# A rational activation spread over four engines: one product moved to GpSimd, two steps kept in PSUM

## The chip, the core and the metric

The kernel runs on one core of a Trainium2 chip. The metric is the device time of one execution in microseconds (us), lower is better. Matmuls run on TensorE (PE), elementwise work on VectorE (DVE), ScalarE (ACT) and GpSimd (POOL); transfers are issued from the queues of SyncE (SP) and GpSimd. Each engine works through its own instructions in the order in which they were issued, and waits on semaphores for the others.

## The reference

Three stages in a row, all in float32, for 8 batches of 3072 rows of 256 columns (24,576 rows):

```python
scores = (1.0 / S) * np.matmul(z, z.transpose(0, 2, 1))   # z: 8 x 3072 x 64
x = u * np.matmul(np.maximum(scores, 0.0) ** 2, v)        # attention, no softmax

# mixture of 8 experts, hidden width 1024: one expert per row, rows with x @ w_skip <= 0 pass through
h = np.maximum(xc[mask] @ w1[e], 0.0)
y[mask] = gate_w[mask, None] * (h @ w2[e])                # out = xc + y

# last stage, hidden width 2048: a rational activation
h = x @ w_in
P = a[0] + a[1] * h + a[2] * h**2 + a[3] * h**3
Q = 1.0 + np.abs(b[0]) * np.abs(h) + np.abs(b[1]) * h**2
out = (P / (Q + 1e-06)) @ w_out
```

## The kernel before

**Precision.** Matmuls take a rounded float32 form ("fp32r"). An operand is split into a high part (rounded) and a low part (the rest), and a product is the sum of three matmuls: high by high, high by low, low by high.

**Ticks and units.** Attention is cut into 8 x 12 x 12 = 1152 *ticks* (256 rows by 256 rows: scores, relu, square, split, product with V). Expert work and the last stage are cut into *units*: 256 hidden columns by 256 rows for an expert; 128 hidden columns by 512 rows for the last stage, which has 48 tiles of 16 units, 768 units in all. The batches are in five groups (1, 2, 2, 2, 1); when a group's attention is through, its expert units run, and its last-stage units are mixed with the ticks of the following groups. At the end there are no ticks left: 152 units of the last stage have the tag "y" (in `munits`, kind `kd`): 8 by themselves, 32 each beside one expert unit of the last group (tag "n"), 16 and then the 96 of the last group alone. Units mixed with ticks have the tag "x".

**One last-stage unit** (`plan_unit`), by the names of its steps. `h` is a PSUM bank of 128 x 512.

- l1a, l1b (TensorE): six matmuls into h (L1077).
- abs (ScalarE, L1257): u = |h|, in a buffer of the ring "mu". p1 (ScalarE, L1258): p = a3 h + a2, ring "mp".
- q0 (GpSimd L1264, or ScalarE L1262, or VectorE): q = b1 u + b0, ring "mq". q1 (VectorE or GpSimd, in the helper at L405): q = q u.
- p2 (VectorE, L1270): p = p h. p3 (VectorE, L1271): h = (p + a1) h, written back to PSUM.
- ln, ex (ScalarE, L1272, L1273): u = exp(-ln(q + CQ)), that is 1 / (q + CQ).
- gh (VectorE, L1274): the high part of the result, (h + a0) u, as fp32r, ring "mgh".
- v (VectorE, L1275): q = (q + CQ) gh. w (VectorE, L1277): q = (h + a0) - q, the rest of the numerator; after it the bank h is free.
- gl (GpSimd or VectorE, L405): the low part, q u, ring "mgl"; after it the buffers of mu and mq are free.
- l2h, l2l (TensorE): eight and four matmuls with gh and gl into the accumulator (L1095).

At the start of a tile its rows are transposed (L1130) and split (ScalarE L1136, VectorE L1139) into "mx"; at its end ScalarE copies the accumulators out (L1158). An expert unit (tag "n" beside a "y") has one pass on ScalarE (L1249) and one on VectorE (L1252).

**The order** is no hand-written list. `Flow.add` collects every step with a start position (the unit's position plus an offset from `LAG` plus a correction from `PAR`), the engines that may do it with a cost each ("D.602s|G1.245t": VectorE 0.602, else GpSimd 1.245), what it comes after, and which buffers of which ring it takes and frees. `Flow.run` plays this list forward at build time, always picks the engine that can begin earliest (within `SLIP` and `AHEAD`), and issues the instructions in that order. "s" and "t" behind a cost mark steps of VectorE and GpSimd which the planner doesn't let run at once.

**Rings that matter here** (`RINGS`): "b" has five PSUM banks (scores, h, transposes), "accA" one (the attention's accumulator; for the last group's experts theirs), "accM" two. "mu" has three buffers, "mp" two, "mq", "mgh" and "mgl" three. "T1" (six) holds attention's transposed z, "wr" (four) raw loads; both are of 128 x 512.

Of the kernel before, what the change touches and what calls it, by code (L numbers as in the profile page):

```python
# [25 lines left out]
    "T4tr.a": -3.5, "T4tr.s": -53.49, "T4tr.t": 16.24, "V.a": -66.78, "V.s": -77.95, "V.t": 93.99, "Vhi.a": -33.49,  # L26
    "Vhi.s": 12.36, "Vhi.t": -16.69, "Vld.a": -9.41, "Vld.s": 8.42, "Vld.t": 24.73, "W.2": 14.14, "W.f": -65.81,
    "W.n": -9.45, "W.v": -1.61, "Wh0.f": -3.7, "Wh1.f": -14.2, "Wl.f": -21.16, "Wo.f": 4.84, "abs.x": -57.27,
    "abs.y": -28.51, "avh.a": 10.74, "avh.t": 5.01, "avl.a": 3.11, "avl.t": -1.16, "ct.a": 71.47, "ct.t": -0.65,
    "ex.x": -7.74, "ex.y": -31.41, "gh.m": -0.03, "gh.n": -11.8, "gh.x": -11.19, "gh.y": -24.37, "gl.m": 122.35,  # L30
    "gl.n": -38.79, "gl.x": -6.33, "gl.y": 6.98, "hi.a": -61.05, "hi.t": -4.31, "l1a.m": 9.14, "l1a.n": 11.77,
    "l1a.x": 3.64, "l1a.y": 5.86, "l1b.m": 10.94, "l1b.n": 4.93, "l1b.x": 1.31, "l1b.y": 5.3, "l2h.m": 8.41,
    "l2h.n": 4.04, "l2h.x": 1.05, "l2h.y": 6.57, "l2l.m": 9.94, "l2l.n": -2.66, "l2l.x": -1.2, "l2l.y": 5.79,
    "ln.x": -3.21, "ln.y": 2.03, "lo.a": 3.28, "lo.t": -9.74, "mhi.1m": -50.66, "mhi.1n": -7.59, "mhi.2x": -7.05,
# [14 lines left out]
    "rt9.t": -93.95, "sq.a": -20.86, "sq.t": -0.93, "u.a": 20.74, "u.s": 47.17, "u.t": -38.96, "v.x": -14.79,  # L49
    "v.y": -38.17, "w.x": -101.31, "w.y": 1.28, "wsc.w": -7.4, "wsc1.f": -6.74, "wscc.w": -34.1, "wsch.w": -20.5,  # L50
    "wscl.w": 18.97,
# [3 lines left out]
SLIP = {"P": 8.95, "A": 0.25, "D": 24.11, "G": 5.02, "Q": 9.0}  # L55
LEAD, TAIL, POST, CARRY, MROW = 24, 8, 56, 1, 8
PE_TICK, PE_UNIT = 1.92, 2.87
# [13 lines left out]
class Flow:  # L71
# [7 lines left out]
    AHEAD = {"P": 10.76, "A": 4.45, "D": 125.36, "G": 8.71, "Q": 0.0}  # L79
# [138 lines left out]
def tile_attn_moe_moe2(  # L218
# [185 lines left out]
    def tt_on(e, *a, **k):  # L404
        (nc.vector if e == "D" else nc.gpsimd).tensor_tensor(*a, **k)  # L405
# [241 lines left out]
    def plan_tick(n):  # L647
# [47 lines left out]
        if ic == NIC - 1 and jp % 2 == 1:  # L695
            sf.append(("T1", ("T1", b, jp // 2)))
        add(at["S"], ("S", n), "P.476", scores, after=sd, takes=[("b", ("S", n))], frees=sf)
# [5 lines left out]
            at["avh"], ("avh", n), "P.952", lambda: av(st["hi"], (0, 1), True, False),  # L703
# [4 lines left out]
            at["avl"], ("avl", n), "P.476", lambda: av(st["lo"], (0,), False, True), after=[("lo", n), ("avh", n)],  # L708
# [499 lines left out]
    def plan_unit(t):  # L1208
        m, fp, xu, kd = munits[t]
        s = {}  # L1210
        ghb, glb = ("ah", "al") if kd == "n" else ("mgh", "mgl")
        flow.tag = kd
# [33 lines left out]
        add(at["l1a"], ("l1a", t), pl1, lambda: l1(0), after=prev + [("m", m.mi, h, "lo") for h in range(m.nh)] + [("W", wn)], takes=[hu])
        add(at["l1b"], ("l1b", t), pl1, lambda: l1(1), after=[("l1a", t)], frees=[("V" if kd == "n" else "mx", ("mx", m.mi))] if last else [])
        if m.kind == 1:
            add(at["gh"], ("gh", t), "A.478", lambda: act(buf("mgh", F32R), s["h"], AF.Relu), after=[("l1b", t)], takes=[(ghb, ("u", t))])  # L1249
            add(  # L1250
                at["gl"], ("gl", t), "D.602",
                lambda: stt(buf("mgl", F32R), s["h"], 0.0, s["gh"].bitcast(F32), op0=ALU.max, op1=ALU.subtract),  # L1252
                after=[("gh", t)], takes=[(glb, ("u", t))], frees=[hu],
            )
        else:

            pt("abs", "A.478", ["l1b"], lambda: act(buf("mu"), s["h"], AF.Abs), ["mu"])  # L1257
# [15 lines left out]
            pt("ex", "A.52", ["ln"], lambda: act(s["u"], s["u"], AF.Exp, scale=-1.0))  # L1273
            pt("gh", "D.663", ["ex", "p3"], lambda: stt(buf("mgh", F32R), s["h"], a0, s["u"], op0=ALU.add, op1=ALU.mult), ["mgh"])  # L1274
            pt("v", "D.602s", ["gh"], lambda: stt(s["q"], s["q"], CQ, s["gh"].bitcast(F32), op0=ALU.add, op1=ALU.mult))  # L1275
            add(
                at["w"], ("w", t), "D.663", lambda: stt(s["q"], s["h"], a0, s["q"], op0=ALU.add, op1=ALU.subtract),  # L1277
                after=[("v", t)], frees=[hu],
            )
# [6 lines left out]
            at["l2l"], ("l2l", t), "P.476", lambda: l2(1),  # L1286
# [191 lines left out]
```

## Time and profile before

| what | value |
|---|---|
| median of 3 runs | 5582.74 us (5581.83 to 5587.68) |
| profiled execution | 5577.05 us, of which the span of instructions 5575.3 |
| busy share of the span: PE, DVE, ACT, POOL | 96%, 81%, 75%, 55% |
| mean granted TensorE clock | 0.994 |
| instructions | 107,018 |

The page's busy shares are means over a span with stages that are limited by different engines; the views below cut it by time. The profiled execution is one run, somewhat faster than the median of the three.

### The profile page before, as it was taken

The numbers are of one execution on the slowest core, as the hardware profiler recorded it, in microseconds if no ns is written. First come the engines' busy times: TensorE is split into PE (matmuls) and PEld (weight loads), VectorE is DVE, ScalarE is ACT, GpSimd is POOL, SyncE is SP. The second block draws the span as 40 slices with busy tenths as digits, with TensorE's granted clock in tenths as the row PEclk, the third lists the DMA queues.
The fourth block names the chain that finished last, engine by engine and source line by source line (L and its number), as shares of the span: only waits on it lengthen the run. The fifth ranks groups of instructions, "written<-read, shape, count | busy, mean of one in ns | idle before, by whom it ended". The sixth has DMA issues, their size and how long they took to land.

```text
span 5575.3 us, 107018 instructions
## 1 busy us (share of the span) xinstructions
PE 5362.4 (96%) x39525; PEld 5027.9 (90%) x39525; DVE 4533.8 (81%) x7470; ACT 4202.2 (75%) x7663; POOL 3090.5 (55%) x4422
## 2 busy tenths in 40 slices
PE   9989999999999999999999999999999999999887
PEld 8989999999899999999899989999988888888666
DVE  6765777774498999899459999999638999998998
ACT  8866888885388888888448888888627888855776
POOL 3433445443256655665235566556526667765887
PEclk9999999999999999999999999999999999999999
DMA  4375111114510110112541010011351000044000
GB/s 136 115 273 218 64 51 42 34 53 176 176 60 32 45 40 31 31 41 76 178 154 36 32 50 27 29 32 48 132 207 63 24 25 20 25 157 140 16 16 17
DMA packets 205545, 435.31 MB, mean 78 GB/s; under 512 B 30094, under 2 KB 129017, under 8 KB 181458
## 3 DMA queue, kind: packets, MB, share of 16 engines
q1 hardware_dynamic: 177746, 360.66, 19.1%
q0 software_dynamic: 27264, 67.71, 3.5%
q8 instruction: 313, 5.13, 0.4%
q14 instruction: 222, 1.82, 0.1%
HBM read 308.56 MB, written 153.22 MB: 83 GB/s over the span
## 4 chain that ended last, share of the span: by engine, by line
PE 70%; DVE 13%; ACT 6%; DMA 4%; issue 4%; POOL 3%; SPq 0%; DVEq 0%; ACTq 0%; POOLq 0%
PE accA L684 24%; PE h L1077 17%; PE accM L1095 16%; PE S L661 4%; PE S L662 4%; DVE mq L1275 3%; DVE mgh L1274 3%; DMA mr<-xs 2%; DVE h L1271 2%; DVE mq L1277 2%; DVE mp L1270 1%; PE lp L773 1%; PE mt L1130 1%; ACT mp L1258 1%; ACT mu L1272 1%
## 5 line engine op out<-in xcount | busy, mean ns | idle before, releaser
L1077 PE MATMUL h<-mx,W 128*128 128x512 f32 x5760 | 1540.7, 400 | 64.1 <-DVE mq L1277 58.9
L684 PE MATMUL accA<-V,ah 128*128 128x256 f32 x9216 | 1270.0, 280 | 13.1 <-ACT ah L409 8.3
L405 POOL TENSOR_TENSOR mgl<-mq,mu 128x512 fp32r<-128x512 f32 x655 | 892.1, 1363 | 692.9 <-DVE mq L1277 395.8
L1077 PEld LDWEIGHTS h<-mx,W 128*128 128x128 f32 x5760 | 1013.5, 190 | 250.6 <-DVE mq L1277 75.3
L684 PEld LDWEIGHTS accA<-V,ah 128*128 128x128 f32 x9216 | 1164.4, 189 | 31.5 <-ACT ah L409 14.5
L1095 PE MATMUL accM<-W,mgh 128*128 128x256 f32 x7680 | 1054.5, 280 | 10.6 <-DVE mgh L1274 6.6
L1095 PEld LDWEIGHTS accM<-W,mgh 128*128 128x128 f32 x7680 | 979.6, 189 | 32.3 <-DVE mgh L1274 8.9
L676 DVE TENSOR_TENSOR al<-S,ah 128x512 fp32r<-128x512 f32 x1152 | 786.3, 683 | 168.4 <-ACT ah L409 143.9
L665 ACT ACTIVATE S<-S 128x512 f32<-128x512 f32 x1152 | 677.9, 588 | 119.2 <-PE S L662 109.5
L684 PE MATMUL accA<-V,al 128*128 128x256 f32 x4608 | 729.7, 281 | 5.9 <-DVE al L676 5.7
L1264 POOL TENSOR_SCALAR mq<-mu,coef 128x512 f32<-128x512 f32 x554 | 458.0, 827 | 473.1 <-ACT mu L1257 467.6
L668 ACT ACTIVATE S<-S 128x512 f32<-128x512 f32 x1152 | 676.0, 587 | 21.8
L1270 DVE TENSOR_TENSOR mp<-mp,h 128x512 f32<-128x512 f32 x768 | 522.3, 680 | 187.0 <-ACT mp L1258 178.1
L1257 ACT ACTIVATE mu<-h 128x512 f32<-128x512 f32 x768 | 458.0, 596 | 271.0 <-PE h L1077 212.2
L409 ACT ACTIVATE ah<-S 128x512 fp32r<-128x512 f32 x996 | 594.9, 598 | 63.3 <-PE accA L684 41.7
L1095 PE MATMUL accM<-W,mgl 128*128 128x256 f32 x3840 | 615.1, 282 | 27.9 <-POOL mgl L405 27.3
L1274 DVE SCALAR_TENSOR_TENSOR mgh<-h,coef,mu 128x512 fp32r<-128x512 f32 x768 | 571.3, 744 | 80.2 <-ACT mu L1273 64.9
L684 PEld LDWEIGHTS accA<-V,al 128*128 128x128 f32 x4608 | 621.4, 189 | 13.5 <-DVE al L676 8.2
L1275 DVE SCALAR_TENSOR_TENSOR mq<-mq,mgh 128x512 f32<-128x512 f32 x768 | 617.4, 805 | 15.7 <-DVE mgh L1274 0.5
L1272 ACT ACTIVATE mu<-mq 128x512 f32<-128x512 f32 x768 | 483.3, 629 | 179.1 <-POOL mq L405 138.6
L1258 ACT ACTIVATE mp<-h,coef 128x512 f32<-128x512 f32 x768 | 595.5, 775 | 23.3 <-DVE h L1271 18.8
L1095 PEld LDWEIGHTS accM<-W,mgl 128*128 128x128 f32 x3840 | 537.3, 189 | 63.4 <-POOL mgl L405 39.7
(157 smaller groups left out, 8466.9 us busy)
## 6 DMA issues: line engine op xcount, KB each, us to landing
W<-wsc SPq DMA_DIRECT2D x96, 1024.0 KB
wsc<-W SPq DMA_DIRECT2D x32, 1024.0 KB
W<-wsc POOLq DMA_DIRECT2D x32, 1024.0 KB
Wv<-wsc SPq DMA_DIRECT2D x64, 512.0 KB
vr<-in_v_dram SPq DMA_DIRECT2D x96, 256.0 KB
xs<-in_u_dram SPq DMA_DIRECT2D x96, 256.0 KB
x<-xs SPq DMA_DIRECT2D x96, 256.0 KB
mr<-x SPq DMA_DIRECT2D x96, 256.0 KB
```

Source lines behind the costliest of these rows:

```text
L405: (nc.vector if e == "D" else nc.gpsimd).tensor_tensor(*a, **k)
L409: act(out, in_, AF.Copy)
L665: act(st["s"], st["s"], AF.Relu, scale=1.0 / S)
L668: act(st["s"], st["s"], AF.Square)
L676: ttt(st["lo"], st["s"], st["hi"].bitcast(F32), op=ALU.subtract)
L684: mm(accs[b, ic][:, it * TT : (it + 1) * TT], lhsT=a[:, jj * TT + it * P : jj * TT + (it + 1) * P], rhs=VV[b, jp][:, vi, jj * D : (jj + 1) ...
L1077: mm(h, lhsT=lw, rhs=rw, start=(k == 0 and i == 0), stop=(k == NK - 1 and i == 2), skip_group_check=True)
L1095: mm(accs_[it // 2][:, it % 2 * TT : (it % 2 + 1) * TT], lhsT=(gh, gl)[part][:, it * P : (it + 1) * P], rhs=w[i][:, 512 + ff * D : 512 + ( ...
L1258: pt("p1", "A.664", ["l1b"], lambda: act(buf("mp"), s["h"], AF.Identity, scale=a3, bias=a2), ["mp"])
L1270: pt("p2", "D.602", ["p1", "abs"], lambda: ttt(s["p"], s["p"], s["h"], op=ALU.mult))
L1274: pt("gh", "D.663", ["ex", "p3"], lambda: stt(buf("mgh", F32R), s["h"], a0, s["u"], op0=ALU.add, op1=ALU.mult), ["mgh"])
L1275: pt("v", "D.602s", ["gh"], lambda: stt(s["q"], s["q"], CQ, s["gh"].bitcast(F32), op0=ALU.add, op1=ALU.mult))
```

## The change

For units of tag "y" alone:

- v goes from VectorE to GpSimd. GpSimd's instruction only multiplies, so the addition of CQ gets a pass of its own, qc, on ScalarE, ahead of ln.
- q1 may only be done by GpSimd.
- w writes its result to h in PSUM, no longer to q; so q is free after w.
- gl is done by VectorE, from h (PSUM) and u; after it h and u are free.
- u takes its buffer from the ring "T1" and q from the ring "wr".
- in the last group, every sixth unit takes its bank h from "accA".

Further, every cost that the planner uses for TensorE's steps, the offsets for "y", its limits `SLIP` and `AHEAD`, and all values of `PAR` are new, so the order of all work may differ.

```diff
-SLIP = {"P": 8.95, "A": 0.25, "D": 24.11, "G": 5.02, "Q": 9.0}
+SLIP = {"P": 11.41, "A": 0.25, "D": 8.5, "G": 24.05, "Q": 9.0}
-PE_TICK, PE_UNIT = 1.92, 2.87
+PE_TICK, PE_UNIT = 1.87, 2.8
-    "y": {"hc": 2.2, "l1a": 0.0, "l1b": 1.46, "abs": 3.3, "p1": 2.17, "q0": 3.9, "q1": 5.31, "p2": 3.21, "p3": 5.4, "ln": 8.99, "ex": 11.23, "gh": 11.96, "v": 13.69, "w": 14.84, "gl": 15.6, "l2h": 20.23, "l2l": 23.37},
+    "y": {"hc": 2.2, "l1a": 0.0, "l1b": 1.4, "abs": 2.9, "p1": 3.5, "q0": 3.6, "q1": 4.6, "p2": 4.4, "p3": 5.2, "qc": 6.1, "ln": 6.8, "ex": 7.5, "gh": 8.2, "v": 9.1, "w": 10.6, "gl": 11.4, "l2h": 12.5, "l2l": 14.5},
-    AHEAD = {"P": 10.76, "A": 4.45, "D": 125.36, "G": 8.71, "Q": 0.0}
+    AHEAD = {"P": 11.11, "A": 4.42, "D": 137.59, "G": 8.94, "Q": 0.0}
...
+        home = {"mgh": ghb, "mgl": glb}
+        if kd == "y":
+            home.update(mu="T1", mq="wr")
...
-        hu = ("b", ("u", t))
+        hb = "accA" if kd == "y" and m.g == NG - 1 and (t - len(munits)) % 6 == 0 else "b"
+        hu = (hb, ("u", t))
...
-            pt("q1", "D.602s|G1.245t", ["q0"], lambda e: tt_on(e, s["q"], s["q"], s["u"], op=ALU.mult))
+            pt("q1", "G1.245t" if kd == "y" else "D.602s|G1.245t", ["q0"], lambda e="G": tt_on(e, s["q"], s["q"], s["u"], op=ALU.mult))
...
+            if kd == "y":
+                pt("qc", "A.52", ["q1"], lambda: act(s["q"], s["q"], AF.Identity, bias=CQ))
+                pt("ln", "A.52", ["qc"], lambda: act(s["u"], s["q"], AF.Ln))
+                pt("ex", "A.52", ["ln"], lambda: act(s["u"], s["u"], AF.Exp, scale=-1.0))
+                pt("gh", "D.663", ["ex", "p3"], lambda: stt(buf("mgh", F32R), s["h"], a0, s["u"], op0=ALU.add, op1=ALU.mult), ["mgh"])
+                pt("v", "G1.245t", ["gh"], lambda: pool_tt(s["q"], s["q"], s["gh"].bitcast(F32), op=ALU.mult))
+                pt("w", "D.663", ["v"], lambda: stt(s["h"], s["h"], a0, s["q"], op0=ALU.add, op1=ALU.subtract), (), ["mq"])
+                pt("gl", "D.602", ["w"], lambda: ttt(buf("mgl", F32R), s["h"], s["u"], op=ALU.mult), ["mgl"], ["mu"], [hu])
+            else:
...

```

## Rows read from the trace of the kernel before

**Rows 1.** The page: busy time of TensorE, share of the span, instructions.
```profile
PE 5362.4 (96%) x39525; PEld 5027.9 (90%) x39525; DVE 4533.8 (81%) x7470; ACT 4202.2 (75%) x7663; POOL 3090.5 (55%) x4422
```

**Rows 2.** Windows: stretch, its length, busy us of each engine, clock, DMA.
```profile
0.00:4905.00 4905.00, 4795.72 (x35930) 4535.97 (x35930) 3918.05 (x6602) 3763.41 (x6953) 2586.78 (x3975) 1.00 0.24 79
1600.00:2600.00 1000.00, 992.45 (x7472) 938.46 (x7471) 912.50 (x1517) 850.87 (x1565) 607.93 (x896) 1.00 0.12 38
3000.00:4000.00 1000.00, 988.99 (x7414) 937.83 (x7413) 919.57 (x1525) 855.25 (x1562) 605.07 (x861) 1.00 0.14 44
4905.00:4940.00 35.00, 29.04 (x162) 24.59 (x162) 32.73 (x54) 19.97 (x35) 26.55 (x40) 0.90 0.42 144
4940.00:5127.00 187.00, 179.59 (x1315) 168.73 (x1316) 160.46 (x231) 101.55 (x169) 97.63 (x99) 0.99 0.52 173
5127.00:5565.00 438.00, 357.78 (x2120) 298.54 (x2119) 422.54 (x586) 316.19 (x505) 379.50 (x310) 0.98 0.05 17
5200.00:5550.00 350.00, 286.51 (x1686) 237.66 (x1686) 338.09 (x469) 257.52 (x412) 308.78 (x252) 0.98 0.05 17
```

**Rows 3.** The chain that ended last, 5200 to 5550 us: shares by line.
```profile
by line: DVE mq L1275 19.4%; DVE mgh L1274 17.3%; issue 15.3%; DVE h L1271 8.8%; DVE mp L1270 6.3%; DVE mq L1277 6.3%; ACT mp L1258 5.1%; ACT mu L1273 5.0%; ACT mu L1272 4.4%; PE h L1077 3.4%; PE accM L1095 3.3%; POOL mq L405 2.0%; PE mt L1
```

**Rows 4.** Groups of VectorE, 5200 to 5550 us: busy us, mean ns, idle before.
```profile
L1275 DVE SCALAR_TENSOR_TENSOR mq<-mq,mgh 128x512 f32<-128x512 f32 x91 | 93.1, 1023 | 3.7
L1274 DVE SCALAR_TENSOR_TENSOR mgh<-h,coef,mu 128x512 fp32r<-128x512 f32 x92 | 68.8, 748 | 6.1 <-ACT mu L1273 1.0
L1271 DVE SCALAR_TENSOR_TENSOR h<-mp,coef,h 128x512 f32<-128x512 f32 x92 | 68.6, 745 | 0.8
L1277 DVE SCALAR_TENSOR_TENSOR mq<-h,coef,mq 128x512 f32<-128x512 f32 x92 | 68.1, 740 | 0.0
L1270 DVE TENSOR_TENSOR mp<-mp,h 128x512 f32<-128x512 f32 x92 | 62.1, 675 | 1.3 <-ACT mp L1258 1.3
L1139 DVE TENSOR_TENSOR mx<-mt,mx 128x512 fp32r<-128x512 f32 x10 | 6.8, 682 | 0.0
```

**Rows 5.** Groups of ScalarE, 5200 to 5550 us.
```profile
L1273 ACT ACTIVATE mu<-mu 128x512 f32<-128x512 f32 x91 | 57.5, 632 | 2.9
L1272 ACT ACTIVATE mu<-mq 128x512 f32<-128x512 f32 x92 | 57.5, 625 | 48.7 <-POOL mq L405 48.7
L1257 ACT ACTIVATE mu<-h 128x512 f32<-128x512 f32 x91 | 54.0, 594 | 21.4 <-POOL mgl L405 12.3 <-PE h L1077 9.0
L1262 ACT ACTIVATE mq<-mu,coef 128x512 f32<-128x512 f32 x24 | 19.6, 817 | 0.8
```

**Rows 6.** Groups of GpSimd, 5200 to 5550 us.
```profile
L405 POOL TENSOR_TENSOR mgl<-mq,mu 128x512 fp32r<-128x512 f32 x92 | 133.5, 1451 | 7.2 <-DVE mq L1277 7.2
L405 POOL TENSOR_TENSOR mq<-mq,mu 128x512 f32<-128x512 f32 x92 | 125.6, 1376 | 4.8
L1264 POOL TENSOR_SCALAR mq<-mu,coef 128x512 f32<-128x512 f32 x68 | 54.3, 799 | 30.0 <-ACT mu L1257 30.0
```

**Rows 7.** Waits, 5200 to 5550 us: us in total, times, longest.
```profile
PE h L1077 <- DVE mq L1277: 40.5, 52, 2.1
...
ACT mu L1257 <- POOL mgl L405: 12.3, 30, 0.4
```

**Rows 8.** Timeline of one round, 5483 to 5497 us: start, duration, instruction.
```profile
5485.40 1.27 POOL L405 TENSOR_TENSOR mq<-mq,mu 128x512 f32<-128x512 f32 x1
5485.60 1.62 DVE L1275 SCALAR_TENSOR_TENSOR mq<-mq,mgh 128x512 f32<-128x512 f32 x1
...
5485.73 1.66 PE L1077 MATMUL h<-mx,W 128*128 128x512 f32 x6 [0.68 <-DVE mq L1277]
5486.63 1.77 POOL L405 TENSOR_TENSOR mgl<-mq,mu 128x512 fp32r<-128x512 f32 x1
...
5488.62 1.31 POOL L405 TENSOR_TENSOR mgl<-mq,mu 128x512 fp32r<-128x512 f32 x1 [0.22 <-DVE mq L1277]
...
5490.54 0.69 DVE L1275 SCALAR_TENSOR_TENSOR mq<-mq,mgh 128x512 f32<-128x512 f32 x1
```

More of the change, by code (lines that the diff above doesn't have):

```diff
@@ L22 @@
 PAR = {
[3 rows of a table removed]
[L26 to L34, printed above, removed]
[14 rows of a table removed]
-    "rt9.t": -93.95, "sq.a": -20.86, "sq.t": -0.93, "u.a": 20.74, "u.s": 47.17, "u.t": -38.96, "v.x": -14.79,
@@ L50 @@
-    "v.y": -38.17, "w.x": -101.31, "w.y": 1.28, "wsc.w": -7.4, "wsc1.f": -6.74, "wscc.w": -34.1, "wsch.w": -20.5,
-    "wscl.w": 18.97,
[3 rows of a table added]
+    "T4tr.a": -1.8, "T4tr.s": -47.01, "T4tr.t": 16.76, "V.a": -69.94, "V.s": -64.87, "V.t": 123.29, "Vhi.a": -23.69,
+    "Vhi.s": -5.03, "Vhi.t": -10.78, "Vld.a": -11.47, "Vld.s": 9.8, "Vld.t": 24.79, "W.2": 15.33, "W.f": -68.79,
+    "W.n": 16.29, "W.v": 1.9, "Wh0.f": -4.83, "Wh1.f": -0.1, "Wl.f": -36.74, "Wo.f": -23.32, "abs.x": -71.17,
+    "abs.y": 0.38, "avh.a": 5.32, "avh.t": 4.27, "avl.a": 1.39, "avl.t": -1.13, "ct.a": 80.47, "ct.t": 17.69,
@@ new lines @@
+    "ex.x": -9.49, "ex.y": -10.28, "gh.m": 2.4, "gh.n": -19.15, "gh.x": -12.57, "gh.y": 8.16, "gl.m": 137.7,
+    "gl.n": -50.97, "gl.x": -3.03, "gl.y": 0.79, "hi.a": -76.03, "hi.t": -4.81, "l1a.m": 8.89, "l1a.n": 9.5,
+    "l1a.x": 3.31, "l1a.y": 6.16, "l1b.m": 10.9, "l1b.n": -2.11, "l1b.x": 0.96, "l1b.y": 3.26, "l2h.m": 6.58,
+    "l2h.n": 4.9, "l2h.x": 0.84, "l2h.y": 11.51, "l2l.m": 8.95, "l2l.n": 0.11, "l2l.x": -1.98, "l2l.y": 5.31,
+    "ln.x": -3.09, "ln.y": 2.23, "lo.a": -20.21, "lo.t": -10.69, "mhi.1m": -13.94, "mhi.1n": -22.71, "mhi.2x": -7.11,
[14 rows of a table added]
@@ L52 @@
+    "rt9.t": -90.19, "sq.a": -29.62, "sq.t": -0.7, "u.a": 8.1, "u.s": 45.54, "u.t": -41.33, "v.x": -14.39, "v.y": -3.41,
+    "w.x": -117.81, "w.y": 2.62, "wsc.w": -5.9, "wsc1.f": -10.91, "wscc.w": -45.45, "wsch.w": -59.53, "wscl.w": 14.6,
 }
@@ L696, in plan_tick @@
             sf.append(("T1", ("T1", b, jp // 2)))
-        add(at["S"], ("S", n), "P.476", scores, after=sd, takes=[("b", ("S", n))], frees=sf)
+        add(at["S"], ("S", n), "P.467", scores, after=sd, takes=[("b", ("S", n))], frees=sf)
         add(at["relu"], ("relu", n), "A.478", relu, after=[("S", n)])
@@ L702, in plan_tick @@
         add(
-            at["avh"], ("avh", n), "P.952", lambda: av(st["hi"], (0, 1), True, False),
+            at["avh"], ("avh", n), "P.932", lambda: av(st["hi"], (0, 1), True, False),
             after=[("hi", n), ("V", b, jp)] + ([("avl", n - 1)] if n else []),
@@ L707, in plan_tick @@
         add(
-            at["avl"], ("avl", n), "P.476", lambda: av(st["lo"], (0,), False, True), after=[("lo", n), ("avh", n)],
+            at["avl"], ("avl", n), "P.466", lambda: av(st["lo"], (0,), False, True), after=[("lo", n), ("avh", n)],
             frees=[("ah", n), ("al", n)] + ([("V", ("V", b, jp))] if ic == NIC - 1 else []),
@@ L1215, in plan_unit @@
         first, last, ff = fp == 0, fp == m.nfp - 1, fp % 2
-        hu = ("b", ("u", t))
+        hb = "accA" if kd == "y" and m.g == NG - 1 and (t - len(munits)) % 6 == 0 else "b"
+        hu = (hb, ("u", t))
         def l1(half):
             if half == 0:
-                s["h"] = bank("b", f"h{t}")
+                s["h"] = bank(hb, f"h{t}")
             if m.nh == 1:
@@ L1234, in buf, with pt @@
         def buf(tag, dt=F32):
-            o = s[tag[1:]] = tl({"mgh": ghb, "mgl": glb}.get(tag, tag), f"{tag}{t}", dt)
+            o = s[tag[1:]] = tl(home.get(tag, tag), f"{tag}{t}", dt)
             return o
-        def pt(n, ops, after, fn, takes=(), frees=()):
+        def pt(n, ops, after, fn, takes=(), frees=(), more=()):
             add(
                 at[n], (n, t), ops, fn, after=[(a, t) for a in after],
-                takes=[(r, ("u", t)) for r in takes], frees=[(r, ("u", t)) for r in frees],
+                takes=[(home.get(r, r), ("u", t)) for r in takes],
+                frees=[(home.get(r, r), ("u", t)) for r in frees] + list(more),
             )
         prev = [("l1a", t - 1)] if t else []
-        pl1 = "P.714" if m.nh == 1 else "P.69"
+        pl1 = "P.7" if m.nh == 1 else "P.696"
         add(at["l1a"], ("l1a", t), pl1, lambda: l1(0), after=prev + [("m", m.mi, h, "lo") for h in range(m.nh)] + [("W", wn)], takes=[hu])
@@ L1268, in plan_unit @@
             pt("q0", "G.78|A.707|D.46s", ["abs"], q0, ["mq"])
-            pt("q1", "D.602s|G1.245t", ["q0"], lambda e: tt_on(e, s["q"], s["q"], s["u"], op=ALU.mult))
+            pt("q1", "G1.245t" if kd == "y" else "D.602s|G1.245t", ["q0"], lambda e="G": tt_on(e, s["q"], s["q"], s["u"], op=ALU.mult))
             pt("p2", "D.602", ["p1", "abs"], lambda: ttt(s["p"], s["p"], s["h"], op=ALU.mult))
             pt("p3", "D.663", ["p2", "abs"], lambda: stt(s["h"], s["p"], a1, s["h"], op0=ALU.add, op1=ALU.mult), (), ["mp"])
-            pt("ln", "A.52", ["q1"], lambda: act(s["u"], s["q"], AF.Ln, bias=CQ))
@@ L1273, in plan_unit @@
[L1273 to L1279, printed above, removed]
@@ L1280, in plan_unit @@
-            pt("gl", "G1.245t|D.602s", ["w"], lambda e: tt_on(e, buf("mgl", F32R), s["q"], s["u"], op=ALU.mult), ["mgl"], ["mu", "mq"])
+            if kd == "y":
[7 more added lines that the diff above has]
+            else:
+                pt("ln", "A.52", ["q1"], lambda: act(s["u"], s["q"], AF.Ln, bias=CQ))
+                pt("ex", "A.52", ["ln"], lambda: act(s["u"], s["u"], AF.Exp, scale=-1.0))
+                pt("gh", "D.663", ["ex", "p3"], lambda: stt(buf("mgh", F32R), s["h"], a0, s["u"], op0=ALU.add, op1=ALU.mult), ["mgh"])
+                pt("v", "D.602s", ["gh"], lambda: stt(s["q"], s["q"], CQ, s["gh"].bitcast(F32), op0=ALU.add, op1=ALU.mult))
+                add(
+                    at["w"], ("w", t), "D.663", lambda: stt(s["q"], s["h"], a0, s["q"], op0=ALU.add, op1=ALU.subtract),
+                    after=[("v", t)], frees=[hu],
+                )
+                pt("gl", "G1.245t|D.602s", ["w"], lambda e: tt_on(e, buf("mgl", F32R), s["q"], s["u"], op=ALU.mult), ["mgl"], ["mu", "mq"])
@@ L1281, in plan_unit @@
         add(
-            at["l2h"], ("l2h", t), "P.952", lambda: l2(0), after=[("gh", t)] + ([("l2l", m.ts[fp - 1])] if fp else []),
+            at["l2h"], ("l2h", t), "P.932", lambda: l2(0), after=[("gh", t)] + ([("l2l", m.ts[fp - 1])] if fp else []),
             takes=[(acc_tag(m), ("m", m.mi, h)) for h in range(m.nh)] if first else [],
@@ L1285, in plan_unit @@
         add(
-            at["l2l"], ("l2l", t), "P.476", lambda: l2(1),
+            at["l2l"], ("l2l", t), "P.466", lambda: l2(1),
             after=[("gl", t), ("l2h", t)] + ([("wsc1", wn)] if wn in range(E * FP1) and w_last[wn] == t else []),
```

34 rows, old and new, of the table PAR are left out of this document.

## The prediction, made before the changed kernel ran

> **What bounds the kernel now.** I read the page first: TensorE is busy in 96% of the span [rows 1]. That is an average over stages, so I cut the span where the work changes [rows 2]. Up to 4905 us attention and expert work run together, and TensorE idles for 109 us of 4905 (4905 - 4795.7). The units that the diff touches, those of tag "y", are the last 152 of 768 rational units: 8 alone (about 4905 to 4940), 32 each beside one unit of the last expert group (to about 5127), and 112 alone up to the end. In the middle piece TensorE is busy for 179.6 of 187 us, so there it is the bound. In the last piece it is busy for 357.8 of 438 us, and VectorE for 422.5.
>
> I take 5200 to 5550 us as the steady part of it: VectorE 338.1 of 350 us, GpSimd 308.8, TensorE 286.5, ScalarE 257.5 [rows 2]; 92 units pass in it (the counts of four of VectorE's five groups, [rows 4]). So a unit takes 350 / 92 = 3.80 us, of which VectorE works 3.675. The chain of waits agrees: its largest shares there are VectorE's, L1275 (v) first with 19.4% [rows 3]. TensorE does wait, 40.5 us at the first matmul of a unit, for L1277, the instruction that gives back a PSUM bank [rows 7]; but that instruction is late because VectorE is full.
>
> Why VectorE is full stands in its groups [rows 4]: p2 0.675, p3 0.745, gh 0.748, w 0.740 and v 1.023 us. v is as wide as the others. The timeline shows what it costs apart from its own work [rows 8]: one v that begins 0.20 us behind a GpSimd product takes 1.62 us, and the next GpSimd product takes 1.77; another v, that waits for nothing, takes 0.69. Products of GpSimd that met no v took 1.27 and 1.31. p2, which reads PSUM and SBUF, averages 0.675 with the same GpSimd work running, so it isn't held.
>
> **The change, step by step** (for a unit alone).
>
> *VectorE.* v leaves: -1.023. gl comes to VectorE. It isn't there in these units now; its nearest rows are p2, the same operation with one operand in PSUM and one in SBUF, 0.675, and the split at L1139 with an fp32r output, 0.682 [rows 4]. I take 0.68. w writes PSUM instead of SBUF: L1271 does that at 0.745, against L1277's 0.740, so nothing. The sum of means is now 0.675 + 0.745 + 0.748 + 0.740 + 1.023 + 0.074 (L1139, 6.8 us over 92 units) = 4.005, and the engine is busy for 3.675, so neighbours overlap by 0.33 a unit. Afterwards it is 4.005 - 1.023 + 0.68 = 3.66, less 0.33 = 3.33 us. Bounds: with no v that waits, all five may overlap by about 0.08 (3.26); if p2-p3 and w-gl stand back to back, where the second needs the first's result, those two overlap nothing (3.41).
>
> *GpSimd.* gl leaves, v comes: the same kind of product, both operands in SBUF. q1 was on GpSimd for 92 of 92 units already. No VectorE instruction with two tensors in SBUF is left in a unit, so the products should fall from 1.451 and 1.376 [rows 6] to about 1.29: busy time 308.8 / 92 = 3.36 becomes 3.36 - 0.16 - 0.09 = 3.11 us. If the lengthening stays, 3.36.
>
> *ScalarE.* One pass more, qc. The Ln with a constant added takes 0.625, q0 on ScalarE with its two columns of coefficients 0.817 [rows 5]; qc has one constant, so 0.625. Busy time 257.5 / 92 = 2.80 becomes 3.34 (0.08 overlaps), or 3.54 at the other price. ScalarE now does q0 in 24 of 92 units; each that goes back to GpSimd moves 0.82 there. Evened out, both stand at some 3.22.
>
> *What hides what.* So VectorE goes from 3.675 to 3.33 and stays the bound, but with two engines close below it, where now they have 0.3 and 0.9 us of slack. Now VectorE idles 0.13 us a unit. I take 0.17 afterwards, since ScalarE (five to six instructions in order) no longer has room to catch up: 3.50 us a unit. With 0.06 and 3.26 it is 3.32; with 0.25 and 3.41 it is 3.66.
>
> *Buffers.* A bank of the unit is given back after gl instead of after w, and the path to there gets qc. What a unit does while it holds the bank is now 1.66 (its matmuls, [rows 8]) + 0.594 + 0.799 + 1.376 + 0.625 + 0.632 + 0.748 + 1.023 + 0.740 = 8.2 us; five banks at 3.80 us a unit allow 19. Afterwards: with products at 1.29, 1.66 + 0.594 + 0.799 + 1.29 + 0.625 + 0.625 + 0.632 + 0.748 + 1.29 + 0.745 + 0.68 = 9.7 us, and five banks at 3.50 allow 17.5. In the last 96 units every sixth takes the attention's bank, which is worth six banks: 21. mu moves from three buffers to six ("T1"), mq from three to four ("wr"); both rings are the attention's, which by then issues no ticks, so I cost the move at nothing. No DMA is added or moved. v now stands in GpSimd's queue; behind it are q0 and q1 of later units and, in the middle piece, the scatters of the expert tiles, for which ScalarE's qc and the output tiles wait; there GpSimd is busy for only 97.6 of 187 us.
>
> *The sum.* The 438 us hold 113 units, counted as above. 113 x (3.80 - 3.50) = -34 us. In the two pieces ahead, TensorE idles 6.0 and 7.4 us, which bounds the gain at 13; I take -4, since in the 187 us VectorE isn't the bound. The last unit's chain gets qc (+0.6), and v and gl change engines at no net cost: +1. The two lists of start positions are also new for all other work. How much the order alone can do I bound by two stretches of the same mixture: 1600 to 2600 leaves TensorE idle for 7.6 us, 3000 to 4000 for 11.0 [rows 2], that is 3.4 us in 1000, or +-17 over 4905; no reason for a sign, so 0. Sum: -37 us. The profiled execution took 5577.05 us around a span of 5575.3, the median of the runs is 5582.74; the sum is a difference, so it goes to the median: **5546 us**. Alone the likeliest case ranges from 113 x 0.48 + 4 = -58 to 113 x 0.14 = -16, narrowed to 5530 to 5566 because both ends need all terms at once.
>
> **Rivals.**
>
> *Full packing.* VectorE's queue is filled without gaps at 3.30 us a unit, and the pieces ahead give 8: -64, 5519. For it: no instruction of VectorE waits for a GpSimd one to end. Against it: three engines above 3.2.
>
> *GpSimd becomes the bound.* If ScalarE can't take any q0, GpSimd has 2 x 1.29 + 0.80 = 3.38 clean, or 2 x 1.376 + 0.80 = 3.55 at today's lengthened product; with 0.13 idle 3.68, so 113 x 0.12 = -14: 5569. For it: v takes twice what it takes on VectorE when nothing is beside it (1.29 against 0.69, [rows 8]). The Trainium skill's GPSIMD Engine Reference, section 4.1, says the same as a rule: a two-input elementwise operation belongs on VectorE, GpSimd being about twice as slow. By that rule alone moving v loses 0.6 us a unit; the trace agrees with the ratio. Against it as a loss: the rows price v on VectorE at 1.023, not 0.69, and gl comes back from GpSimd in exchange.
>
> *The order elsewhere, or the gaps, take it back.* At 3.75 us a unit with a new order worth nothing, or at 3.60 with +17: about 5580, no change to be measured.
>
> *Slower: the bank.* Today a unit spends 19 - 8.2 = 10.8 us of its hold on waits in queues. If these grow with the number of hand-overs (GpSimd's v between two VectorE instructions, qc between GpSimd and ScalarE: nine steps become eleven), the hold is 9.7 + 13.2 = 22.9 us. On six banks that is 3.82 a unit, on five 4.58: over 96 and 17 units, 2 + 13 = +15 us: 5598. It decides from a hold of 6 x 3.80 = 22.8 us on. Against it: queues are long now because VectorE is full, and mu's three buffers, for which ScalarE's first pass waits [rows 7], become six.
>
> **How the numbers follow.** Likeliest case 0.52, full packing 0.17, GpSimd the bound 0.13, no change 0.09, slower 0.09. The first three are faster by more than 0.2% (11 us, about what a measurement here can tell from no change): 0.82, less 0.01 for their slow ends: 0.81 faster, 0.10 same, 0.09 slower. The range of 5520 to 5578 us reaches from full packing to the edge of no change; outside are half of full packing, the slower case and part of the unchanged one.
>
> **What would show it.** Right: in the steady part VectorE still has the highest busy share, some 95%, at about 3.5 us a unit; gl on VectorE near 0.68 and w near 0.745; GpSimd's two products near 1.29, none near 1.7; ScalarE above 90%; TensorE's wait for a bank now ends on gl. Wrong: products still at 1.4 (something else of VectorE holds GpSimd), gl or w well above 0.75, VectorE below 90% while TensorE waits for gl longer than 40 us (the bank), or a gain or loss that lies ahead of 4905 us (the order).

## The result, and the profile after

The changed kernel takes 5535.45 us (median of 4 runs); the kernel before, run again beside it, has a median of 5583.42. One of the four runs took 6764.53 us at a mean granted TensorE clock of 0.719; it is in that median but not in the ratio, and the other three took 5530.0 to 5538.0. The ratio is 0.991 with a 95% interval of 0.989 to 0.9929: 0.9% faster, 48 us, where 37 were forecast. A second series gave 5530.63 against 5586.91, ratio 0.990 (0.9884 to 0.9917).

The profiled execution took 5530.01 us with a span of 5528.3, that is 47.0 less than the span before. Four instants in TensorE's timeline split the difference: the last matmul of a tick, the first and the last of the last group's expert units, and the last of all.

| stretch | before, us | after, us | difference |
|---|---|---|---|
| start to the last tick's matmul | 4896.3 | 4911.2 | +14.9 |
| to the first expert unit of the last group | 35.6 | 38.9 | +3.3 |
| beside those expert units | 199.6 | 190.0 | -9.6 |
| lone units, to the last matmul | 433.9 | 377.8 | -56.1 |

So the lone units gave more than the whole gain, and some of it was lost ahead of them. The first instant in both profiles, the kernel before first (start, duration):

```profile
4895.63 0.62 PE L684 MATMUL accA<-V,al 128*128 128x256 f32 x4
```

```profile
4910.55 0.62 PE L683 MATMUL accA<-V,al 128*128 128x256 f32 x4
```

The windows after (columns as in [rows 2]; the third and fourth lines are the two lower stretches of the table, the last a steady part of the lone units):

```profile
0.00:4905.00 4905.00, 4787.04 (x35825) 4532.41 (x35826) 3933.89 (x6588) 3743.91 (x6897) 2608.91 (x3994) 1.00 0.23 79
4911.20:4950.00 38.80, 30.35 (x174) 26.54 (x173) 33.06 (x56) 26.59 (x48) 31.45 (x45) 0.87 0.27 84
4950.00:5140.00 190.00, 187.44 (x1404) 177.96 (x1403) 148.13 (x229) 126.99 (x216) 120.18 (x116) 1.00 0.56 187
5140.00:5518.00 378.00, 333.40 (x2083) 292.13 (x2081) 369.80 (x581) 351.03 (x607) 353.08 (x315) 1.00 0.06 20
5175.00:5500.00 325.00, 289.94 (x1800) 254.00 (x1799) 319.33 (x499) 308.62 (x535) 308.50 (x275) 1.00 0.06 19
```

In the steady part 98 units pass in 325 us (the count of gh below): 3.32 us a unit, against 3.80. VectorE is busy for 319.3 of 325 us (98%), ScalarE and GpSimd for 95% each; before, these three were at 97%, 74% and 88% [rows 2]. Beside the expert units TensorE is busy for 187.4 of 190 us; before, for 179.6 of 187.

The groups of 5175 to 5500 us (line, engine, operation, count, busy us, mean ns, idle before), first VectorE with gh, p3, w, p2 and gl, then ScalarE's qc, then GpSimd's q1, v and q0:

```profile
L1283 DVE SCALAR_TENSOR_TENSOR mgh<-h,coef,mu 128x512 fp32r<-128x512 f32 x98 | 72.9, 743 | 2.1 <-ACT mu L1282 1.8
L1277 DVE SCALAR_TENSOR_TENSOR h<-mp,coef,h 128x512 f32<-128x512 f32 x98 | 73.3, 748 | 0.8
L1285 DVE SCALAR_TENSOR_TENSOR h<-h,coef,mq 128x512 f32<-128x512 f32 x97 | 72.8, 751 | 0.0
L1276 DVE TENSOR_TENSOR mp<-mp,h 128x512 f32<-128x512 f32 x98 | 66.3, 677 | 2.7 <-ACT mp L1264 2.7
L1286 DVE TENSOR_TENSOR mgl<-h,mu 128x512 fp32r<-128x512 f32 x97 | 66.0, 681 | 0.1
...
L1280 ACT ACTIVATE mq<-mq 128x512 f32<-128x512 f32 x98 | 60.9, 621 | 2.9 <-POOL mq L404 2.5
L1268 ACT ACTIVATE mq<-mu,coef 128x512 f32<-128x512 f32 x20 | 16.1, 806 | 0.0
...
L404 POOL TENSOR_TENSOR mq<-mq,mu 128x512 f32<-128x512 f32 x99 | 128.0, 1298 | 5.8 <-ACT mq L1268 2.0
L1284 POOL TENSOR_TENSOR mq<-mq,mgh 128x512 f32<-128x512 f32 x97 | 126.2, 1302 | 8.1 <-DVE mgh L1283 8.1
L1270 POOL TENSOR_SCALAR mq<-mu,coef 128x512 f32<-128x512 f32 x79 | 61.7, 781 | 4.8 <-ACT mu L1263 4.8
```

Compare with [rows 4, 6]: no row of VectorE is above 0.76 us any more, and GpSimd's products are at 1.30 instead of 1.38 and 1.45. The waits of the same stretch show that TensorE hardly waits for a bank any more, 5.7 us instead of 40.5 [rows 7], and waits longer for gl as an operand, 28.2 us instead of 11.8:

```profile
PE accM L1094 <- DVE mgl L1286: 28.2, 30, 2.1
...
PE h L1076 <- DVE mgl L1286: 5.7, 5, 1.5
```

The timeline (start, duration) shows GpSimd's q1 and v back to back, with VectorE's gl and p2 beside them, neither side lengthened:

```profile
5486.55 1.30 POOL L404 TENSOR_TENSOR mq<-mq,mu 128x512 f32<-128x512 f32 x1
5486.55 0.74 DVE L1283 SCALAR_TENSOR_TENSOR mgh<-h,coef,mu 128x512 fp32r<-128x512 f32 x1
...
5487.21 0.68 DVE L1286 TENSOR_TENSOR mgl<-h,mu 128x512 fp32r<-128x512 f32 x1
...
5487.81 0.68 DVE L1276 TENSOR_TENSOR mp<-mp,h 128x512 f32<-128x512 f32 x1
5487.81 1.30 POOL L1284 TENSOR_TENSOR mq<-mq,mgh 128x512 f32<-128x512 f32 x1
```

### The profile page after: what moved, and what is told of

The parts are those of the page before. It is cut to its first block, busy times and chain, and to the rows that moved or that the text cites. A ratio compares the mean times of both kernels' runs of the same rounds, so it can differ in the third digit from the quotient of the medians.

```text
span 5528.3 us, 106807 instructions
## 1 busy us (share of the span) xinstructions
PE 5344.4 (97%) x39525; PEld 5034.9 (91%) x39525; DVE 4491.1 (81%) x7460; ACT 4254.6 (77%) x7776; POOL 3119.6 (56%) x4471
## 4 chain that ended last, share of the span: by engine, by line
PE 73%; DVE 14%; ACT 5%; issue 3%; POOL 3%; DMA 2%; SPq 0%; DVEq 0%; POOLq 0%; ACTq 0%
PE accA L683 24%; PE h L1076 18%; PE accM L1094 17%; PE S L660 4%; PE S L661 4%; DVE mp L1276 2%; DVE h L1277 2%; DVE mq L1291 2%; DVE mgh L1290 1%; DVE h L1285 1%; PE accM L1084 1%; PE h L1065 1%; PE lp L772 1%; DMA wr<-in_moe_w_dram 1%; PE mt L1129 1%
## 5 line engine op out<-in xcount | busy, mean ns | idle before, releaser
L1076 PE MATMUL h<-mx,W 128*128 128x512 f32 x5760 | 1522.5, 398 | 21.6 <-DVE mq L1293 11.8
L683 PEld LDWEIGHTS accA<-V,ah 128*128 128x128 f32 x9216 | 1168.4, 189 | 24.4 <-ACT ah L408 11.8
L404 POOL TENSOR_TENSOR mgl<-mq,mu 128x512 fp32r<-128x512 f32 x484 | 655.5, 1356 | 627.2 <-DVE mq L1293 380.7
L408 ACT ACTIVATE ah<-S 128x512 fp32r<-128x512 f32 x971 | 579.9, 597 | 47.2 <-PE accA L683 22.2
L661 PE MATMUL S<-T,T 128*128 128x256 f32 x2304 | 590.3, 281 | 0.0
L1277 DVE SCALAR_TENSOR_TENSOR h<-mp,coef,h 128x512 f32<-128x512 f32 x768 | 572.8, 747 | 3.8
L404 POOL TENSOR_TENSOR mq<-mq,mu 128x512 f32<-128x512 f32 x405 | 541.2, 1338 | 40.4 <-ACT mq L1268 15.4
```

Of the source, the lines that this page charges most:

```text
L408: act(out, in_, AF.Copy)
L661: mm(o, lhsT=lw, rhs=T4[b, ic], start=False, stop=(jj == 1), skip_group_check=True)
L683: mm(accs[b, ic][:, it * TT : (it + 1) * TT], lhsT=a[:, jj * TT + it * P : jj * TT + (it + 1) * P], rhs=VV[b, jp][:, vi, jj * D : (jj + 1) ...
L1076: mm(h, lhsT=lw, rhs=rw, start=(k == 0 and i == 0), stop=(k == NK - 1 and i == 2), skip_group_check=True)
```

## The experiments

In each, the planner lays out the order anew, so the edit is followed by a slightly or strongly different order. The planner's numbers stay those of the changed kernel, or of the kernel before, and aren't made anew for the edit; part of a loss can therefore be the order's, as the runs under "Steps or numbers?" show. Times a unit are counted by gh between 5200 and 5500 us unless another stretch is named. The five runs with a time but no ratio are single executions.

**Is it the PSUM operand?** gl from two SBUF tensors, everything else as changed:

```diff
-pt("w", "D.663", ["v"], lambda: stt(s["h"], s["h"], a0, s["q"], op0=ALU.add, op1=ALU.subtract), (), ["mq"])
-pt("gl", "D.602", ["w"], lambda: ttt(buf("mgl", F32R), s["h"], s["u"], op=ALU.mult), ["mgl"], ["mu"], [hu])
+pt("w", "D.663", ["v"], lambda: stt(s["q"], s["h"], a0, s["q"], op0=ALU.add, op1=ALU.subtract))
+pt("gl", "D.602", ["w"], lambda: ttt(buf("mgl", F32R), s["q"], s["u"], op=ALU.mult), ["mgl"], ["mu", "mq"], [hu])
```

> The changed kernel with w written to q in SBUF and gl taken from q and u, both in SBUF, on VectorE; everything else, the time at which the bank is given back too, as in the changed kernel. Theory P (two SBUF tensors on VectorE and a GpSimd product hold each other up; keeping one in PSUM is what avoids it): gl at 0.9 to 1.1 us instead of 0.68, GpSimd's products at 1.36 to 1.45 instead of 1.30, 3.6 to 3.8 us a lone unit, total 5570 to 5590. Rival (only the change of engine counts): gl at 0.69, products at 1.30, total 5530 to 5540.

Measured: 5580.87 us, 81 units in 300 us, 3.70 a unit; the lone units take 423.8 us, against 377.8 in the changed kernel and 433.9 before. The groups (VectorE's gl, GpSimd's v and q1), 5200 to 5500 us:

```profile
L1286 DVE TENSOR_TENSOR mgl<-mq,mu 128x512 fp32r<-128x512 f32 x80 | 81.5, 1018 | 0.0
```

```profile
L1284 POOL TENSOR_TENSOR mq<-mq,mgh 128x512 f32<-128x512 f32 x81 | 122.0, 1506 | 7.3 <-DVE mgh L1283 7.3
L404 POOL TENSOR_TENSOR mq<-mq,mu 128x512 f32<-128x512 f32 x81 | 117.2, 1455 | 3.8 <-ACT mq L1268 1.1
```

and two pairs from its timeline, one with gl behind a product, one with a product behind gl:

```profile
5303.68 1.28 POOL L404 TENSOR_TENSOR mq<-mq,mu 128x512 f32<-128x512 f32 x1
5303.75 1.77 DVE L1286 TENSOR_TENSOR mgl<-mq,mu 128x512 fp32r<-128x512 f32 x1
```

```profile
5301.81 0.76 DVE L1286 TENSOR_TENSOR mgl<-mq,mu 128x512 fp32r<-128x512 f32 x1
5302.00 1.73 POOL L1284 TENSOR_TENSOR mq<-mq,mgh 128x512 f32<-128x512 f32 x1
```

In the first, gl began 0.07 us behind the product and ended 0.56 us after it. In the second, the product began 0.19 us behind gl and ended 1.16 us after it. The same holds for all such pairs of the 300 us: 58 gl that began during a product ended 0.55 to 0.58 us after it, and 65 products that began during a gl ended 1.14 to 1.18 us after it. That is theory P, with the products (1.455 and 1.506) above its 1.36 to 1.45: the later of the two gets its work done only once the earlier has ended, whichever engine it is on. The Trainium skill's SBUF — State Buffer, section "SBUF: two separate sides", states it as an exclusive lock on a pair of ports that VectorE and GpSimd share, held for a whole instruction, and counts a VectorE operation with two SBUF inputs among those that take it; the trace agrees, with 1.77 against 0.68 us for gl.

Over the stretch that costs 0.34 us on gl and 0.16 to 0.20 on each product, and it gives back 46 of the 56 us that the lone units had won. The edit also holds q's buffer until gl; the longer gl explains the loss without that, since VectorE's busy time a unit rises from 3.26 to 3.62 us, 0.36 of the 0.38 lost:

```profile
5200.00:5500.00 300.00, 251.09 (x1511) 217.19 (x1509) 293.55 (x415) 263.06 (x447) 285.04 (x224) 0.98 0.06 18
```

**Are the buffers needed?** u and q in their old rings:

```diff
-            home.update(mu="T1", mq="wr")
+            pass
```

> The changed kernel with u and q of the lone units in their old rings (mu three, mq three buffers) in place of the attention's six and four. From the pass that fills u to gl, which frees it, a unit works for 0.59 + 0.78 + 1.30 + 0.62 + 0.63 + 0.63 + 0.74 + 1.30 + 0.75 + 0.68 = 8.0 us; three buffers at 3.32 us a unit allow 10.0, so 1.9 us of waits in queues. Theory R (the rings are needed: waits in three queues that are 95% full are longer than that): 3.5 to 3.8 us a unit, total 5555 to 5595. Rival (the change of engines alone makes the time): 3.35 us or less, total 5530 to 5540.

Measured: 5586.5 us, 78 units in 300, 3.85 a unit. The window and the wait for u's buffer (by abs, for the gl that frees it):

```profile
5200.00:5500.00 300.00, 241.16 (x1435) 207.63 (x1434) 267.01 (x401) 261.41 (x433) 239.75 (x212) 0.98 0.06 18
```

```profile
ACT mu L1263 <- DVE mgl L1286: 14.1, 24, 1.4
```

No engine is full any more: VectorE 89%, ScalarE 87%, GpSimd 80%. The total is in theory R's range, the rate somewhat beyond its upper price of 3.8; the rival falls. The wait shown, 14.1 us, is a third of the 41 us lost in this stretch; the rest would have to come from what is late because of it (q0 waits 25.0 us for abs), or from an order that was made for six and four buffers. The run doesn't separate these.

**The buffers alone**, with the old steps and the old numbers:

```diff
-            pt("q1", "G1.245t" if kd == "y" else "D.602s|G1.245t", ["q0"], ...)
+            pt("q1", "D.602s|G1.245t", ["q0"], ...)
...
-            if kd == "y":
+            if kd == "never":
                 pt("qc", "A.52", ["q1"], ...)
```

(the choice of rings and bank for the y units stays as changed.)

> The kernel before, old steps and old planner numbers, with the attention's rings for u and q of the y units and its bank for every sixth unit of the last group alone. Theory (VectorE is full at 3.67 us of 3.80 a unit, so more buffers can't help; they are needed only once VectorE has less to do): 3.7 to 3.85 us a unit, v still above 1.0 us, total 5568 to 5585. Rival (the buffers alone make the gain): 3.5 us or less, total 5535 to 5550.

Measured: 5590.41 us, 91 units in 350 us from 5200 on, 3.85 a unit; VectorE busy for 339.7 of 350. v averages 0.90 us here, less than forecast, but 14 q1 and 11 gl have come to VectorE instead:

```profile
L1292 DVE SCALAR_TENSOR_TENSOR mq<-mq,mgh 128x512 f32<-128x512 f32 x91 | 80.7, 896 | 0.2
L405 DVE TENSOR_TENSOR mq<-mq,mu 128x512 f32<-128x512 f32 x14 | 13.6, 972 | 2.9 <-ACT mq L1269 2.2 <-POOL mq L1271 0.6
L405 DVE TENSOR_TENSOR mgl<-mq,mu 128x512 fp32r<-128x512 f32 x11 | 7.9, 715 | 0.0
```

These 25 instructions are 21.5 us of VectorE's work, which the planner's order put there. So the buffers alone won nothing in this order, and the rival's rate of 3.5 isn't there; what they would win with the 25 left on GpSimd wasn't run. In the orders tried, steps and buffers won only together.

**The bank.** Without every sixth unit's bank:

```diff
-        hb = "accA" if kd == "y" and m.g == NG - 1 and (t - len(munits)) % 6 == 0 else "b"
+        hb = "b"
```

> The changed kernel without the attention's bank for every sixth unit of the last group. A unit works for 9.7 us while it holds its bank; five banks at 3.32 us allow 16.6, so 6.9 us of waits. Theory (the bank is not what limits): within 5 us of the changed kernel, 5530 to 5540. Rival (the slower case's mechanism: the hold grows with the hand-overs until the banks limit): 3.6 us or more, total 5565 or more, and TensorE's wait for gl at the first matmul of a unit above 30 us.

Measured: 5545.31 us, 87 units in 300, 3.45 a unit; TensorE's wait for gl at a unit's first matmul is 9.8 us. The time lies 5 us above the theory's range and 20 below the rival's, so neither number is met. The sixth bank is worth 0.13 us a unit; the rival's mechanism, banks that limit, isn't there at five.

**GpSimd as the bound.** q0 of these units on GpSimd alone:

```diff
-            pt("q0", "G.78|A.707|D.46s", ["abs"], q0, ["mq"])
+            pt("q0", "G.78" if kd == "y" else "G.78|A.707|D.46s", ["abs"], lambda e="G": q0(e), ["mq"])
```

> The changed kernel with q0 of the y units on GpSimd alone (now ScalarE does 20 of 99). GpSimd then works for 2 x 1.30 + 0.78 = 3.38 us a unit, VectorE 3.26, ScalarE 0.16 less. Theory (GpSimd becomes the bound, at its clean price): GpSimd 97% or more busy, 3.42 to 3.55 us a unit, total 5540 to 5556. Rival (VectorE stays the bound): 3.35 us or less, total within 5 us of the changed kernel.

Measured: 5554.49 us, 86 units in 300, 3.49 a unit:

```profile
5200.00:5500.00 300.00, 262.83 (x1601) 231.35 (x1600) 285.93 (x442) 261.10 (x453) 281.91 (x257) 0.97 0.06 20
```

The time is the theory's, its mechanism isn't shown: GpSimd is at 94%, not 97, and VectorE still at 95%, as in the rival. Both work for about 3.3 us a unit and neither is filled to the end. That ScalarE takes a fifth of the q0 is worth some 20 us.

**Steps or numbers?** The diff also replaced every number of the planner. First the new steps with the old numbers (start corrections, `SLIP`, `AHEAD`, lengths, and TensorE's costs, which the cut leaves out; the starts of the y units in `LAG` stay the new ones), and then, with the signs exchanged and on the kernel before, the old steps with the new numbers:

```diff
 PAR = {
-    "S.a": 2.58, "S.t": -2.68, "T1.a": -69.45, "T1.s": 2.31, ...
+    "S.a": 5.12, "S.t": -3.04, "T1.a": -59.25, "T1.s": -0.83, ...
...
+    "qc.y": 0.0,
 }
-SLIP = {"P": 11.41, "A": 0.25, "D": 8.5, "G": 24.05, "Q": 9.0}
+SLIP = {"P": 8.95, "A": 0.25, "D": 24.11, "G": 5.02, "Q": 9.0}
...
-PE_TICK, PE_UNIT = 1.87, 2.8
+PE_TICK, PE_UNIT = 1.92, 2.87
...
-    AHEAD = {"P": 11.11, "A": 4.42, "D": 137.59, "G": 8.94, "Q": 0.0}
+    AHEAD = {"P": 10.76, "A": 4.45, "D": 125.36, "G": 8.71, "Q": 0.0}
```

> The new steps and rings of the units alone, with all planner numbers of the kernel before (start corrections, limits, TensorE costs, unit length); only the offsets of the y units are the new ones, since qc needs one. Theory A (the steps make the gain, the new numbers cost some 15 us ahead of the last stage): the ticks end at about 4896 us as before, the lone units run at 3.3 to 3.5 us each, total 5515 to 5535. Rival B (the new numbers make the gain by a better order, the steps little): 5565 to 5585.

> The old steps with all new planner numbers (old offsets of the y units). Theory A: ticks end at about 4911 us, then 3.8 us a lone unit as before, total 5590 to 5605, slower than before. Rival B: ticks end at 4911, lone units near 3.4, total 5535 to 5555.

Both times lie far outside both theories' ranges. The new steps with the old numbers take 6592.8 us (ratio 1.1805, 1.1786 to 1.1825), the old steps with the new ones 5679.32 (1.017, 1.0154 to 1.0187). In the first, between 5600 and 6500 us, 90 units pass in 900 us, 10.0 a unit:

```profile
5600.00:6500.00 900.00, 493.66 (x1650) 388.65 (x1650) 334.02 (x459) 285.94 (x469) 293.88 (x269) 0.61 0.02 6
```

```profile
POOL mq L1285 <- DVE mgh L1284: 490.6, 90, 7.1
ACT mu L1264 <- PE h L1077: 483.0, 77, 7.9
PEld accM L1095 <- DVE mgh L1284: 399.6, 90, 5.4
```

Nothing is full; every engine stands for an instruction whose input is late, because the queues hold the steps of successive units in an order in which hardly two units overlap. In all 90 units GpSimd's v waits for gh, and in nearly all of them a later unit's q0 and q1 stand right behind it in the queue.

TensorE's mean granted clock is 0.61 there, between its levels of 1.2 GHz (0.5) and 2.4 GHz (1.0), after stretches in which it waited. Its matmuls stand in the chain, since abs waits 483.0 us for them, so the lower clock adds to the 10.0 us: the six first matmuls and the eight of gh fill 2.5 and 2.0 us a unit, against 1.5 and 1.1 in the changed kernel, so by these busy times an estimated 1.9 of the 6.7 us more a unit are the clock's.

In the second run, between 5200 and 5600 us, all 86 counted q1 went to VectorE, and GpSimd waits 130.0 us for w with gl, 4.65 us a unit:

```profile
POOL mgl L405 <- DVE mq L1277: 130.0, 28, 5.8
```

Neither theory A nor B holds in its plain form: steps and start corrections belong together.

Then the new steps with old numbers and the new corrections of the y units alone, the 17 keys of `PAR` that end in ".y" (against the run with the old numbers throughout):

```diff
-    "gh.x": -11.19, "gh.y": -24.37, "gl.m": 122.35,
+    "gh.x": -11.19, "gh.y": 8.16, "gl.m": 122.35,
...
```

> As the first, and with the new start corrections of the y units alone. Theory A: ticks end at 4896, lone units at 3.3 us, total 5515 to 5525, faster than the changed kernel by 10 to 20. Rival C (the 15 us ahead are what the fast end is bought with: work that the new order has done earlier): the end is then slower by as much, total 5530 to 5540. Rival B: 5565 or more.

Measured: 5556.61 us, ratio 0.9955 (0.9941 to 0.997). The ticks end at 4897.5 and 89 lone units take 300 us (3.37), but the piece beside the expert units takes 219.9 us, so the total is in no theory's range. The next two runs have the new corrections of those expert units too ("gh.n", "mtr.1n", "W.v" and their like) and those that prepare the rows of the y tiles (the six that end in ".2y", "mtr.2y" for one); the second of the two also has `SLIP`, `AHEAD` and the unit length switched to the new ones at the last tick:

```diff
-    "gh.m": -0.03, "gh.n": -11.8,
+    "gh.m": -0.03, "gh.n": -19.15,
...
-                lim = min(lim, s + SLIP[e])
+                lim = min(lim, s + (SLIP2 if now > self.turn else SLIP)[e])
...
-                while todo and todo[-1][0] <= now + self.AHEAD[e]:
+                while todo and todo[-1][0] <= now + (self.AHEAD2 if now > self.turn else self.AHEAD)[e]:
...
-        clock[0] += PE_UNIT
+        clock[0] += PE_UNIT if len(x_tick) < NA else 2.8
...
     acc_of = {}
+    flow.turn = x_tick[NA - 1]
```

> As the run with the new start corrections of the y units alone, and with the new corrections of the expert units beside them too; everything ahead keeps the old numbers. Theory D (the 30 us that run lost, it lost beside the expert units, whose corrections belong together with those of the y units): the ticks end at 4897, the piece beside the expert units takes 190 to 195 us in place of 220, lone units 3.32 to 3.40, total 5520 to 5530. Rival (the limits of the planner and its unit length make that piece): 5550 to 5560 again.

> As the one with the new corrections from the y units on, and with the new limits (SLIP and AHEAD) and the new unit length once the last tick's position has passed; the old ones up to it. Theory D and its rival both: 5515 to 5525, if the 15 us ahead of the ticks' end can be kept together with the new end; theory D gives no gain over the run without the new limits beyond 5 us, the rival 25 us or more. Rival C (the new order buys its end with the 15 us): 5530 or more.

Measured: 5526.7 us (ratio 0.9902, 0.9885 to 0.9918) and 5521.61 (0.9895, 0.9879 to 0.9912); the piece beside the expert units is back at 191.9 us in the first. That is theory D's price for that piece; since the corrections of the y tiles' rows changed with those of the expert units, which of the two it takes isn't shown. The new limits give 5 us more, far from the rival's 25. The kernel before ran at 5577.37 in that series, so the last one, with a gain of 56 us, was run once more beside the changed kernel:

> The changed kernel once more, on the same chip as the next one. Its ticks should end at 4910 to 4917 us again, as in every profile with the new numbers so far, and lone units take 3.3 us; 40 to 55 us faster than before.

> The kernel with the old numbers up to the last tick and the new ones from there, beside the changed kernel. Theory D (the new order costs some 13 us ahead of the ticks' end): 8 to 18 us faster than the changed kernel, ticks end at 4894 to 4909. Rival (that difference is the spread between executions): within 5 us of the changed kernel.

Measured: 5530.63 and 5530.03 us, ratios 0.990 (0.9884 to 0.9917) and 0.9903 (0.9886 to 0.9919). The changed kernel's gain, 56 us, lies at the upper edge of the 40 to 55 expected. Between the two there is no difference: theory D's gain isn't there, its rival holds, and no version beats the changed kernel beyond the intervals. The last matmul of a tick in the two profiles, the changed kernel first:

```profile
4913.88 0.62 PE L683 MATMUL accA<-V,al 128*128 128x256 f32 x4
```

```profile
4902.80 0.62 PE L684 MATMUL accA<-V,al 128*128 128x256 f32 x4
```

The ticks ended 11 us sooner with the old numbers, and the rest took 614.3 us instead of 605.1.

**The ticks' end over all profiles.** With the new numbers ahead of it: 4911.2, 4914.7, 4916.5, 4909.9, 4915.7, 4914.5, 4916.0 us, mean 4914.1. With the old ones: 4896.3, 4903.9, 4897.5, 4908.7, 4893.9, 4901.6, 4903.4, mean 4900.8. By that instant TensorE has done 35,870 matmuls in all fourteen, and the same ones, counted by tile. So the new order does the same matmuls some 13 us later. The seven old ones have, by tiles, one order on TensorE but for the last 28 matmuls, and still spread by 15 us.

## Why the prediction was right, point by point

- **VectorE, 3.33 us a unit**: mis-sized a little. 319.3 us over 98 units are 3.26, the lower bound. The parts were right: gl 0.681 (0.68), w 0.751 (0.745). What was off is the overlap, 0.33 taken over from before: it became 0.40. A waiting v isn't the reason, since it overlapped its neighbours by 0.08 us like any other. What grew is the share of VectorE's instructions that begin before the one ahead has ended, 349 of 466 neighbours before and 459 of 496 after.
- **GpSimd**: products 1.298 and 1.302 (1.29), busy 308.5 / 98 = 3.15 (3.11). That no VectorE instruction of a unit holds it any more was the central step, and the run with gl from SBUF shows it. The prediction took the 1.27 us product of [rows 8] for one that met no v; a v did begin 0.20 us behind it, and only the later of the two was lengthened.
- **ScalarE**: qc 0.621 (0.625), busy for 308.6 / 98 = 3.15 a unit (3.22 evened out); it does 20 of 99 q0, where it did 24 of 92.
- **Idle time of VectorE, 0.17 us a unit**: this term was mis-sized most. It is 3.32 - 3.26 = 0.06, the lower bound again. The lone units gave 56 us where the sum had 34 - 1 = 33; the rate is that of the rival "full packing" (3.30), which got a chance of 0.17 because three engines above 3.2 seemed too close. They are that close (3.26, 3.15 and 3.15), and VectorE idles for less than before.
- **Buffers**: I costed their move at nothing and gave them no gain either. No cost shows, but without them the new steps won nothing (3.85 us a unit, in an order not made for it), so the gain rests on both.
- **The bank**: going down to five costs 0.13 us a unit, and TensorE's wait for a bank is then 9.8 us in 300; the slower rival stays far from its point of decision.
- **The pieces ahead, -4**: +3.3 and -9.6, together -6.3.
- **The order, 0 within 17**: +13 in the mean over profiles. The price of 0 was off, the bound held; a loss ahead of 4905 us was one of the prediction's own signs of being wrong, and it came beside its signs of being right, of which only the rate (3.32, not 3.5) was off. That it can't be kept apart from the gain in the end (the last pair) I hadn't seen; the reason stays open: the shorter rest of the new numbers is spread over all three stretches, 3.5, 3.3 and 2.4 us.

In sum two terms were off by -23 and +13, and they met in a total 11 us below the forecast, within its range. The mechanism was right; that the total came so close is partly luck, as the two errors have opposite signs.

## What to carry to other kernels

Count a VectorE instruction at what it costs beside the GpSimd work that runs with it, and look first for operands that can stay in PSUM: here one operand more in SBUF cost 0.38 us on 3.32 a unit. When three engines come within a few per cent of each other, try more buffers for the longest chain together with the new steps: here the steps alone gained nothing. And an order that was made for one set of steps is part of that set: the new steps with the old planner numbers were 18% slower, so compare versions only with an order made for each.

## What the runs showed of the hardware beyond that

- The lengthening isn't only that of products: with gl from SBUF, nine of GpSimd's tensor_scalar (q0) began during a gl and took 1.11 to 1.31 us, where the others take 0.76 to 0.79.
- With the same order on TensorE up to there, the ticks' end came at 4893.9 us in one execution and at 4908.7 in another; a difference of 10 us between two single profiles ahead of that point says nothing here.
